# A three-stage fp32 kernel on one core: the first pass ordered by a list scheduler written in the kernel, attention two head pairs at a time

## The chip, the cores and the metric

The kernel runs on one core of a Trainium2 chip. The metric is the device time of one execution in microseconds (us), the median of several. TensorE (PE) multiplies matrices, VectorE (DVE) and ScalarE (ACT) work elementwise, GpSimd (POOL) fills constants, and SyncE (SP) issues nearly all transfers between HBM and the on-chip memory SBUF. PE writes to PSUM, eight banks of accumulators.

## The reference, cut to what matters

A linear attention over 8 batches, 8 heads, 576 tokens and 64 dimensions (softmax of q over the dimensions, softmax of k over the tokens) is followed by two feed-forward layers, 512 to 2048 to 512, over the 4608 tokens. Inputs are 32-bit floats except the weights of the layers, which arrive as 64-bit floats.

```python
q_s = softmax(q, axis=-1)                              # q, k, v: (8, 8, 576, 64)
k_s = softmax(k, axis=2)
kv = np.einsum('bhsd,bhse->bhde', k_s, v)
attn_out = np.einsum('bhsd,bhde->bhse', q_s, kv)
x = attn_out.transpose(0, 2, 1, 3).reshape(4608, 512)
h = x @ w_in                                           # (512, 2048)
x = (h * (1.0 / (1.0 + np.exp(-1.702 * h)))) @ w_out   # (2048, 512)
h = x @ w2_in
g = np.where(h >= 1, h, np.where(h <= -1, 0.0, (h + 1) ** 2 / 4))
return g @ w2_out
```

## The kernel before, in words

Every operand of the large products is split into a high and a low part in the fp32r type (`split`), and a product is three matmuls: high by high, high by low, low by high. The work has four stages: the first pass (attention and `x @ w_in`, activation, result `g0` to HBM), then `out_pass` for the first `w_out` (L308), `pass_in` for the second `w_in` (L463), and `out_pass` again. The last three use a seven-product scheme on quadrants and are not touched, except for two scalings in `post` (L392): the first pass hands on twice the activation, and `keep` and `more` halve it.

The first pass has 9 blocks of 512 tokens and 16 steps a block, 144 steps. Step s is `gemm1` (L794): 12 matmuls of 128x128 by 512 columns for one 128-column slice m of `w_in`. Two steps fill one of two PSUM bank pairs (`hps`); then `act` (L807) runs a Tanh on ACT and a multiply-add on DVE and stores 512 KB of `g0`. In the first 16 steps the weight slices are loaded as 64-bit words and converted (`conv`, one ACT and three DVE instructions; then `split`) into `w_in`, which stays on chip.

Beside the matmuls of block j run the attention pieces of block j + 1 (`chain`, L824). They go by head pair `hp`, four of them: `load_k`, `load_v`, `k_max` (maximum over tokens held on a partition), `k_col` (transpose on PE, maximum on DVE), `k_sub` (transpose back and subtract), `k_exp`, and `k_v`: ten fp32 matmuls that put k'v and the sum of k in the two column halves of one bank, then a scaled copy of two 64x64 blocks into a block-diagonal 128x128 `kv`. For the queries they go by 128 tokens, four tiles a block: `load_q`, `q1` (maximum, subtract), `q1e` (Exp), `q2` (sum, reciprocal, multiply), `q3` (four transposes on PE, a copy to `qT`). `q4` multiplies `qT` of one head pair with `kv`, 512 columns in one or two segments where the block spans two batches, and splits the result into `xh`, `xl`. Block 8 is the last; in block 7 only queries are prepared, since eight batches are done.

From step 17 on, eight sets of the other weights are loaded, converted and turned into the seven combinations that the later stages need (`weight_sets`), one set in 12 steps; the results go to HBM (`wp_*`). Towards the end the first of them come back (`load_weight`), and with block 8 the quadrants of `g0` are loaded for the second pass.

The order: `at(s, f)` notes that piece f is issued after step s; the list is sorted, and the pieces are issued between the steps in that order (L871 on). The framework then orders the instructions of each engine by itself, with priority by this order, so a small matmul can stand in the middle of a step. Every engine runs its instructions strictly in the order that results. The pieces for block 0 come ahead of the first step, q and v of the first two head pairs by ACT's queue, the other loads by SP's.

## Time and profile before

| | us |
|---|---|
| median of 3 runs | 1571.37 |
| lowest and highest | 1567.52, 1572.13 |
| the profiled execution | 1570.93 |
| its span, first to last instruction | 1569.1 |
| its mean granted TensorE clock, as a share of full speed | 0.996 |

The profile is one execution. A page gives the busy time of each engine; the trace behind it is asked for stretches of time, groups of instructions, waits and instructions in order of time. A busy PE is not a PE at its peak, since the ends of matmuls are modelled and they overlap; so the distance between the starts of two matmuls is read, not their length. Where a wait is put down to an instruction, that one came last.

### The profile page before, as it was taken

Reading aid. Unit: us, or ns where it says so; the run is one execution under the profiler, and the core shown is the slowest. Engines: PE = TensorE matmul, PEld = TensorE weight load, DVE = VectorE, ACT = ScalarE, POOL = GpSimd, SP = SyncE. Lnnn points to the kernel's source line nnn. Section 1 sums busy time; section 2 is a strip of 40 time slices with the busy share of each in tenths; the row PEclk is TensorE's granted clock in tenths of the full one; section 3 lists DMA queues with packets and bytes.
Section 4 is the critical chain, followed back from the end, with each engine's and each line's share of the span. In section 5 each row is a group of like instructions: output and inputs, shape, how many; then the busy total and the mean of one; then the engine's idle time right before and its main releaser. Section 6 shows DMA issues by size and latency. Waiting matters only on the chain. (4 is left out here: it accounts for less than half of the span.)

```text
span 1569.1 us, 20971 instructions
## 1 busy us (share of the span) xinstructions
PE 1536.9 (98%) x7748; PEld 1307.6 (83%) x7748; DVE 1163.6 (74%) x1546; ACT 821.9 (52%) x1058; POOL 8.8 (1%) x45
## 2 busy tenths in 40 slices
PE   4999999999999999999999999999999999999998
PEld 2677788777787888888999888888999888888998
DVE  6999887787843678686778577777664879696885
ACT  5555445544523444444445687778776544343442
POOL 0000000000000000000000000000000000000000
PEclk8999999999999999999999999999999999999999
DMA  8787788887787751615268766566744963535341
GB/s 234 212 258 266 263 271 274 267 271 252 251 293 274 289 201 68 213 56 178 71 199 310 294 223 241 202 231 228 259 160 169 426 201 136 159 110 144 111 121 41
DMA packets 249080, 330.65 MB, mean 211 GB/s; under 512 B 129553, under 2 KB 193041, under 8 KB 246289
## 3 DMA queue, kind: packets, MB, share of 16 engines
q1 hardware_dynamic: 243696, 328.09, 62.0%
q10 hardware_dynamic: 5280, 1.21, 0.4%
q8 instruction: 61, 1.00, 0.3%
q14 instruction: 43, 0.34, 0.1%
HBM read 190.84 MB, written 138.41 MB: 210 GB/s over the span
## 5 line engine op out<-in xcount | busy, mean ns | idle before, releaser
L107 ACT ACTIVATE s<-s 128x1024 fp32r<-128x1024 f32 (+2 forms) x363 | 325.1, 901 | 377.9 <-PE z L359 149.7
L108 DVE TENSOR_TENSOR s<-s,s 128x1024 fp32r<-128x1024 f32 (+2 forms) x363 | 369.0, 1023 | 152.7 <-PE zx L359 66.1
L359 PE MATMUL z<-s,w 128*128 128x512 f32 (+1 forms) x1920 | 399.8, 367 | 0.4 <-DVE s L108 0.4
L359 PEld LDWEIGHTS z<-s,w 128*128 128x128 f32 x1920 | 349.5, 188 | 45.9 <-DVE s L108 0.8
L359 PE MATMUL zx<-s,w 128*128 128x512 f32 (+1 forms) x1440 | 300.8, 367 | 0.7 <-DVE s L377 0.7
L359 PEld LDWEIGHTS zx<-s,w 128*128 128x128 f32 x1440 | 262.2, 188 | 34.6 <-DVE s L377 1.0
L803 PE MATMUL hps<-xh,w 128*128 128x512 f32 x576 | 236.2, 410 | 3.0 <-ACT w L107 3.0
L805 PE MATMUL hps<-xh,w 128*128 128x512 f32 x576 | 226.9, 394 | 0.7 <-DVE w L108 0.6
L804 PE MATMUL hps<-xl,w 128*128 128x512 f32 x576 | 226.2, 393 | 0.0
L121 DVE TENSOR_TENSOR s<-s,s 128x1024 f32<-128x1024 f32 (+2 forms) x196 | 204.7, 1058 | 12.7 <-DMA s<-g 8.9
L485 PE MATMUL z<-s,w 128*128 128x512 f32 (+1 forms) x960 | 207.2, 367 | 0.0
L485 PEld LDWEIGHTS z<-s,w 128*128 128x128 f32 x960 | 175.0, 188 | 22.9 <-DVE s L501 0.4
L485 PE MATMUL zx<-s,w 128*128 128x512 f32 (+1 forms) x720 | 158.5, 368 | 1.8 <-DVE s L121 1.6
L485 PEld LDWEIGHTS zx<-s,w 128*128 128x128 f32 x720 | 130.7, 188 | 20.8 <-DVE s L121 3.8
L813 DVE SCALAR_TENSOR_TENSOR sg<-sg,hps 128x1024 f32<-128x1024 f32 x72 | 87.7, 1218 | 62.2 <-ACT sg L812 59.6
L803 PEld LDWEIGHTS hps<-xh,w 128*128 128x128 f32 x576 | 108.8, 189 | 28.8 <-ACT w L107 4.3
L805 PEld LDWEIGHTS hps<-xh,w 128*128 128x128 f32 x576 | 108.2, 188 | 25.6 <-DVE w L108 2.4
L812 ACT ACTIVATE sg<-hps 128x1024 f32<-128x1024 f32 x72 | 73.8, 1025 | 101.4 <-PE hps L805 96.8
L804 PEld LDWEIGHTS hps<-xl,w 128*128 128x128 f32 x576 | 108.5, 188 | 20.9 <-issue 0.6
L500 ACT ACTIVATE s<-s 128x1024 f32<-128x1024 f32 (+1 forms) x80 | 77.6, 971 | 1.6
L499 ACT ACTIVATE s<-s,half 128x1024 f32<-128x1024 f32 (+1 forms) x40 | 42.4, 1060 | 23.6 <-DVE s L121 23.6
L501 DVE SCALAR_TENSOR_TENSOR s<-s,s 128x1024 f32<-128x1024 f32 (+1 forms) x40 | 44.7, 1117 | 12.6 <-ACT s L500 11.2
(79 smaller groups left out, 1074.2 us busy)
## 6 DMA issues: line engine op xcount, KB each, us to landing
s<-g SPq DMA_DIRECT2D x96, 512.0 KB, 5.1
g<-sg SPq DMA_DIRECT2D x72, 512.0 KB, 3.2
w<-wp_out SPq DMA_DIRECT2D x14, 2048.0 KB, 14.8
g<-s SPq DMA_DIRECT2D x48, 512.0 KB, 3.0
s<-g SPq DMA_DIRECT2D x48, 384.0 KB, 4.0
wp_out<-w SPq DMA_DIRECT2D x28, 512.0 KB, 4.0
wp_in<-w SPq DMA_DIRECT2D x28, 512.0 KB, 3.7
w<-wp_in SPq DMA_DIRECT2D x7, 2048.0 KB, 8.7
```

The lines of the kernel that those rows point to most:

```text
L107: first = nc.scalar.activation(out=hi, in_=src, func=ACTF.Copy)
L108: return nc.vector.tensor_tensor(out=lo, in0=src, in1=hi.bitcast(FP32), op=ALU.subtract), first
L121: return nc.vector.tensor_tensor(out=o, in0=x, in1=y, op=op)
L359: nc.tensor.matmul(out=z[:, m, :n], lhsT=a, rhs=b[:, c, :], start=(p in OPENS and i == 0 and c == 0 and x == 0), stop=(i == 3 and c == 1 a ...
L485: nc.tensor.matmul(out=z[:, m, :n], lhsT=a, rhs=b[:, c, :], start=(p in OPENS and c == 0 and x == 0), stop=(c == 1 and x == 2), skip_group ...
L500: nc.scalar.activation(out=t, in_=t, func=ACTF.Square)
L501: nc.vector.scalar_tensor_tensor(out=t, in0=h, scalar=1.0, in1=t, op0=ALU.max, op1=ALU.min)
L803: nc.tensor.matmul(out=hps, lhsT=wh, rhs=xh[:, kk, :], start=(kk == 0), stop=False)
L804: nc.tensor.matmul(out=hps, lhsT=wh, rhs=xl[:, kk, :], start=False, stop=False)
L805: nc.tensor.matmul(out=hps, lhsT=wl, rhs=xh[:, kk, :], start=False, stop=(kk == KD - 1))
L812: nc.scalar.activation(out=sg, in_=hps, func=ACTF.Tanh, scale=0.851)
L813: nc.vector.scalar_tensor_tensor(out=sg, in0=sg, scalar=1.0, in1=hps, op0=ALU.add, op1=ALU.mult)
```

## The change

The pieces of the first pass become entries of a `Plan`: an engine, a price in ns, a rank, names that it reads and writes, bytes' time on the transfer engines (`moves`) and PSUM banks that it takes or gives back. `Plan.order` is a list scheduler: it goes through time, takes on each engine the piece that can start first, and among those the one of lowest rank. The pieces are then issued in that order under `manual_schedule`, so the framework no longer reorders PE, DVE, ACT and SP.

```diff
+class Plan:
+    LATE = {"PE": 190, "DVE": 130, "ACT": 130, "SP": 1900}
+    def __init__(self, banks):
+        self.pieces, self.banks = [], banks
+    def add(self, engine, ns, rank, fn, reads=(), writes=(), moves=0, take=0, give=0):
+        self.pieces.append((rank, len(self.pieces), engine, ns, fn, reads, writes, moves, take, give))
+    def order(self):
+        pieces = sorted(self.pieces, key=lambda x: x[:2])
+        wrote, read, needs, after = {}, {}, [], [[] for _ in pieces]
+        for n, (_, _, _, _, _, reads, writes, _, _, _) in enumerate(pieces):
+            deps = {wrote[r] for r in reads if r in wrote}
+            for w in writes:
+                deps |= {wrote[w]} if w in wrote else set()
+                deps |= set(read.pop(w, ()))
+                wrote[w] = n
+            for r in reads:
+                read.setdefault(r, []).append(n)
+            deps.discard(n)
+            needs.append(len(deps))
+            for d in deps:
+                after[d].append(n)
+        since = [0] * len(pieces)
+        free = dict.fromkeys(self.LATE, 0)
+        open_to = {e: [n for n, x in enumerate(pieces) if x[2] == e and not needs[n]] for e in free}
+        banks, moved, out = [0] * self.banks, 0, []
+        def when(e, n):
+            take = pieces[n][8]
+            if take > len(banks):
+                return None
+            return max(free[e], since[n], sorted(banks)[take - 1] if take else 0)
+        while len(out) < len(pieces):
+            best = None
+            for e, ns in open_to.items():
+                starts = [(t, n) for n in ns if (t := when(e, n)) is not None]
+                if starts:
+                    first = min(t for t, _ in starts)
+                    pick = min(n for t, n in starts if t <= first)
+                    if best is None or first < best[0]:
+                        best = first, e, pick
+            start, e, n = best
+            _, _, _, ns, _, _, _, moves, take, give = pieces[n]
+            open_to[e].remove(n)
+            free[e] = done = start + ns
+            if take:
+                banks = sorted(banks)[take:]
+            if moves:
+                moved = done = max(done, moved) + moves
+            done += self.LATE[e]
+            banks += [done] * give
+            for m in after[n]:
+                since[m] = max(since[m], done)
+                needs[m] -= 1
+                if not needs[m]:
+                    open_to[pieces[m][2]].append(m)
+            out.append((start, n))
+        return [pieces[n][4] for _, n in sorted(out)]
+def now(rank, engine, ns, fn, *_, **__):
+    fn()
```

Attention goes by half the heads (two head pairs, `p`) for k and v and by 256 tokens, two of them on a partition, for q. `k_v` has the same ten matmuls for a head pair, two head pairs in one bank, with the 64 leftover tokens padded to 128 rows; the scaled copy of kv is one DVE instruction, and `kv` is no longer block-diagonal. `q4` has four 64x64 matmuls for two head pairs, in the four quarters of PE's array.

```diff
+        def load_k(b, p, eng=nc.sync):
+            kt = st["k", b, p] = kpool.tile([P, 4, KR + 1, D], FP32, tag="k", name="kt")
+            src = k[b, 4 * p:4 * p + 4]
+            nc.gpsimd.memset(kt[KT:, :, KR], LOWEST)
+            eng.dma_start(out=kt[:, :, :KR], in_=src[:, :KR * P].rearrange("h (p r) d -> p h r d", r=KR))
+            eng.dma_start(out=kt[:KT, :, KR], in_=src[:, KR * P:].rearrange("h p d -> p h d"))
...
+        def k_sub(b, p):
+            kt = st["k", b, p]
+            top = st["pb"].rearrange("p u (h o d) -> p (u h) o d", h=2, o=1)
+            for r0, r1 in ((0, 2), (2, KR + 1)):
+                nc.vector.tensor_tensor(
+                    out=kt[:, :, r0:r1], in0=kt[:, :, r0:r1], in1=top.to_broadcast([P, 4, r1 - r0, D]),
+                    op=ALU.subtract,
+                )
...
+        def k_v(b, p):
+            kt, vt = st["k", b, p], v_t[p]
+            pk = st["pk"] = ps_a.tile([P, 2, D + 1], FP32, tag="a", name="pk")
+            for u in range(2):
+                for r in range(KR + 1):
+                    for h in range(2):
+                        nc.tensor.matmul(
+                            out=pk[h * D:(h + 1) * D, u, :],
+                            lhsT=kt[:, 2 * u + h, r, :],
+                            rhs=vt[:, 2 * u + h, r, :],
+                            start=(r == 0),
+                            stop=(r == KR),
+                            tile_position=(0, h * D),
+                            skip_group_check=True,
+                        )
+        def k_out(b, p):
+            pk = st["pk"]
+            rs = sm.tile([P, 2, 1], FP32, tag="rs", name="rs")
+            nc.vector.tensor_scalar(out=rs, in0=pk[:, :, D:], scalar1=EPS, scalar2=None, op0=ALU.add)
             nc.vector.reciprocal(out=rs, in_=rs)
-            kv = kv_t[b % 2]
-            for j in range(2):
-                o = slice(j * D, (j + 1) * D)
-                nc.scalar.activation(out=kv[o, hp, o], in_=pk[o, :D], func=ACTF.Copy, scale=rs[o])
+            tt(kv_t[b % 2][:, 2 * p:2 * p + 2, :], pk[:, :, :D], rs.to_broadcast([P, 2, D]), ALU.mult)
...
+        def q_exp(t):
+            nc.scalar.activation(out=heads(t), in_=heads(t), func=ACTF.Exp)
...
+        def q4(j, pair):
+            px = [ps_a.tile([P, TB], FP32, tag="a", name="px") for _ in range(2)]
             for off, n, b, s in segs(j * TB, TB, S):
+                for c in range(2):
+                    for r in range(2):
+                        rows = slice(r * D, (r + 1) * D)
+                        nc.tensor.matmul(
+                            out=px[r][c * D:(c + 1) * D, off:off + n],
+                            lhsT=kv_t[b % 2][rows, pair + 2 * c, :],
+                            rhs=st["qT", j][rows, pair + 2 * c, off:off + n],
+                            start=True,
+                            stop=True,
+                            tile_position=(r * D, c * D),
+                            skip_group_check=True,
+                        )
+            for r in range(2):
+                st["px", 2 * pair + r] = px[r]
```

`q1`, `q_exp`, `q2` and `k_max` handle twice the width an instruction. The query and key Exp of a half become one piece, `exps`. The activation becomes one function, and the two scalings of the second pass go:

```diff
         def act(s):
+            sg = st["sg", s] = sgp.tile([P, 2, TB], FP32, tag="sg", name="sg")
+            nc.scalar.activation(out=sg, in_=h_ps[s], func=ACTF.Gelu_apprx_sigmoid)
...
-            nc.scalar.activation(out=sg, in_=hps, func=ACTF.Tanh, scale=0.851)
-            nc.vector.scalar_tensor_tensor(
-                out=sg, in0=sg, scalar=1.0, in1=hps, op0=ALU.add, op1=ALU.mult
-            )
-            nc.sync.dma_start(out=g0_dram[j][m // 2], in_=sg)
```

The order of heads in x changes, so a weight slice is loaded with two transfers of 64 partitions. The pieces, with their ranks and prices:

```diff
+        def attention(j, c0):
             b = j if j < B else None
...
+                put(-5, "SP", 560 * (2 if j else 1), lambda t=t: load_q(t), step(u - 6), nf, moves=1750)
...
+                    put(-6, "SP", 1120, lambda p=p: load_k(b, p), step(u - 7), nk, moves=1800)
+                    put(-1, "SP", 2800, lambda p=p: load_v(b, p), step(u - 2), nv, moves=2600)
+                    put(0, "DVE", 1350, lambda p=p: k_max(b, p), nk, ("mx",))
+                    put(1, "PE", 230, k_col, ("mx",), ("pa",), take=1)
+                    put(1.2, "DVE", 350, k_top, ("pa",), ("mc",), give=1)
+                    put(2, "PE", 230, k_row, ("mc",), ("pb",), take=1)
+                    put(2.2, "DVE", 1500, lambda p=p: k_sub(b, p), ("pb",), nk, give=1)
+                    put(5, "PE", 1400, lambda p=p: k_v(b, p), nk + nv, ("pk",), take=1)
+                    put(5.2, "DVE", 500, lambda p=p: k_out(b, p), ("pk",), (("kv", b % 2, p),), give=1)
+                put(0.2, "DVE", 2400, lambda t=t: q1(t), nf, nq)
+                def exps(t=t, p=p):
+                    q_exp(t)
+                    if b is not None:
+                        k_exp(b, p)
+                put(3, "ACT", (1000 + (1200 if b is not None else 0)) + (2560 if j else 0), exps, (),
+                    nq + (nk if b is not None else ()))
+                put(4.2, "DVE", 2650, lambda t=t: q2(t), (), nq)
+                for r in range(2):
+                    put(6, "PE", 480, lambda t=t, r=r: q3(t, r), nq, (("pt", r),), take=1)
+                    put(6, "ACT", 520, lambda t=t, r=r: q_out(t, r), (("pt", r),), (("qT", p, r),), give=1)
+            qT = tuple(("qT", p, r) for p in range(2) for r in range(2))
+            kv = tuple(("kv", bb, p) for bb in range(2) for p in range(2))
+            for pair in range(2):
+                add("PE", 1000, c0 + 12, lambda pair=pair: q4(j, pair), qT + kv, (("px", pair),), take=2)
+                for r in range(2):
+                    c = 2 * pair + r
+                    add("ACT", 530, c0 + 12.5, lambda c=c: x_hi(j, c), (("px", pair),), (("xh", x, c),))
+                    add("DVE", 620, c0 + 12.6, lambda c=c: x_lo(j, c), (("px", pair), ("xh", x, c)),
+                        (("xl", x, c),), give=1)
+        for m in range(NM):
+            weight(m)
+        for j in range(NB):
+            attention(j, (j - 1) * NM)
...
+        room = (("room", 0),)
+        add("PE", 0, s0 - 0.01, last_block,
+            step(s0 - 1) + tuple((n, 0, c) for n in ("xh", "xl") for c in range(4)), room)
+        for rank, fn in (
+            (0, lambda: g0.load(0, "11")), (4, lambda: g0.load(0, "12")), (8, lambda: g0.load(0, "22")),
+            (14, lambda: load_weight(w_out1, "out1", 2)), (14.1, lambda: g0.load(0, "21")),
+        ):
+            add("SP", 1300, s0 + rank, fn, room + step(s0 + int(rank) - 1), (), moves=5000)
...
+            add("DVE", 1300, s0 + 13 + i, lambda i=i: ready0(i), room + step(s0 + 11 + i), ())
+        for s in range(NB * NM):
+            j, m = divmod(s, NM)
+            hb, gb = ("hps", s // 2 % 2), ("sg", s // 2 % 3)
+            x = tuple((n, j % 2, c) for n in ("xh", "xl") for c in range(4))
+            add("PE", 2720, s, lambda s=s: gemm1(s), x + (("wh", m), ("w", m)) + (room if j == NB - 1 else ()),
+                (hb,) + step(s))
+            if s % 2:
+                add("ACT", 950, s + 1.05, lambda s=s: act(s), (hb,), (gb,))
+                add("SP", 420, s + 1.6, lambda s=s: store_g(s), (gb,), (), moves=1270)
...
+        engines = {mybir.EngineType.PE, mybir.EngineType.DVE, mybir.EngineType.Activation, mybir.EngineType.SP}
+        with tc.manual_schedule(engines=engines):
+            for fn in plan.order():
+                fn()
```

The prices of `conv`, of the weight sets and of the weights' splits follow the same manner. Weight sets come every 14 steps (`s0 = NM + 1 + 14 * i`), each gated by the step two before its rank; the first three combinations of the first `w_out` come back at ranks 130, 133 and 136 (before: after step 113). All loads of block 0 go by SP's queue. GpSimd no longer clears `kv` and pads one k tile for two head pairs.

## Rows read from the trace of the kernel before

**Rows 1.** The page, part 1: busy time, share of the span, instructions.
```profile
PE 1536.9 (98%) x7748; PEld 1307.6 (83%) x7748; DVE 1163.6 (74%) x1546; ACT 821.9 (52%) x1058; POOL 8.8 (1%) x45
```

**Rows 2.** Stretches, cut where a block's first matmul starts; columns in the first line.
```profile
core 0: us, PE busy (x) PEld busy (x) DVE busy (x) ACT busy (x) POOL busy (x), PEclk, DMA share, GB/s
0.00:40.11 40.11, 18.91 (x113) 11.17 (x113) 26.01 (x69) 21.32 (x62) 3.55 (x21) 0.83 0.87 236
40.11:101.26 61.15, 57.51 (x314) 43.17 (x313) 59.36 (x120) 35.59 (x59) 0.80 (x4) 1.00 0.78 234
...
210.29:264.64 54.35, 54.35 (x313) 43.82 (x312) 43.40 (x78) 27.32 (x41) 1.24 (x4) 1.00 0.82 267
...
430.58:479.54 48.96, 48.96 (x217) 38.99 (x216) 23.64 (x36) 15.31 (x20) 0.00 (x0) 1.00 0.70 254
479.54:523.08 43.54, 43.54 (x194) 36.04 (x193) 12.13 (x10) 10.23 (x10) 0.00 (x0) 1.00 0.92 326
```

**Rows 3.** Waits of PE, 40 to 530 us: us in total, times, longest.
```profile
PE hps L803 <- ACT w L107: 3.0, 4, 1.2
```

**Rows 4.** PE in order of time, end of block 7: start, us, what.
```profile
473.10 0.60 PE L764 MATMUL pt<-ident,qt 128*128 128x128 f32 x4
474.47 3.62 PE L774 MATMUL px<-qT,kv 128*128 128x512 f32 x8
```

**Rows 5.** PE in order of time, a k chain between matmuls of block 0.
```profile
57.17 0.39 PE L805 MATMUL hps<-xh,w 128*128 128x512 f32 x1
57.48 0.95 PE L709 MATMUL pk<-v,kt 128*64 128x65 f32 x20
58.37 0.33 PE L681 MATMUL pa<-ident,mx 128*128 128x128 f32 x1
58.45 0.48 PE L803 MATMUL hps<-xh,w 128*128 128x512 f32 x1
58.77 0.40 PE L804 MATMUL hps<-xl,w 128*128 128x512 f32 x1
```

**Rows 6.** Groups of ACT instructions by form: busy us, mean ns, idle before.
```profile
L812 ACT ACTIVATE sg<-hps 128x1024 f32<-128x1024 f32 x72 | 73.8, 1025 | 101.4 <-PE hps L805 96.8 <-DMA g<-sg 4.2
...
L700 ACT ACTIVATE kt<-kt 128x640 f32<-128x640 f32 x32 | 23.6, 737 | 21.0 <-DVE kt L691 20.4
...
L724 ACT ACTIVATE kv<-pk,rs 64x64 f32<-64x64 f32 x64 | 19.6, 307 | 23.9 <-DVE rs L720 19.6 <-DVE qz L753 3.9
...
L745 ACT ACT_TABLE_LOAD x1 | 1.3, 1283 | 9.4 <-DMA qt<-in_q_dram 9.4
```

**Rows 7.** Groups of DVE instructions by form.
```profile
L813 DVE SCALAR_TENSOR_TENSOR sg<-sg,hps 128x1024 f32<-128x1024 f32 x72 | 87.7, 1218 | 62.2 <-ACT sg L812 59.6 <-DMA wp_in<-w 1.6 <-DMA g<-sg 0.9
...
L108 DVE TENSOR_TENSOR w<-w 128x512 fp32r<-128x512 f32 x64 | 43.5, 683 | 1.4 <-ACT w L107 1.3
...
L755 DVE TENSOR_TENSOR qt<-qt,qz 128x512 f32<-128x512 f32 x36 | 24.7, 687 | 0.3
```

**Rows 8.** The start in order of time: first DVE pass, `q4`, first matmul.
```profile
3.83 0.42 DVE L673 TENSOR_TENSOR m<-kr 128x256 f32<-128x256 f32 x1 [3.83 <-DMA kr<-in_k_dram]
...
34.41 6.26 PE L774 MATMUL px<-qT,kv 128*128 128x512 f32 x8 [0.88 <-ACT qT L769]
40.11 0.79 PE L803 MATMUL hps<-xh,w 128*128 128x512 f32 x1
```

**Rows 9.** Three more stretches: ahead of the first matmul, and around the seam.
```profile
30.00:40.00 10.00, 9.12 (x35) 4.93 (x36) 6.70 (x16) 5.30 (x11) 0.00 (x0) 0.52 0.92 254
...
460.00:480.00 20.00, 20.00 (x86) 15.03 (x85) 12.06 (x19) 8.08 (x12) 0.00 (x0) 1.00 0.35 132
...
540.00:560.00 20.00, 20.00 (x90) 16.55 (x89) 15.42 (x14) 9.90 (x10) 0.00 (x0) 1.00 0.08 32
```

**Rows 10.** DMA issues by group: count, KB each, median us to landing.
```profile
g<-sg SPq DMA_DIRECT2D x72, 512.0 KB, 3.2
```

450 lines of the change are left out of this document (178 added, 272 removed).

## The prediction

> **What bounds the kernel now.** First the page's busy table: TensorE (PE) is busy 98% of the span [rows 1], so a gain has to shorten PE's own stream or its start. Next the stretches of the first pass, cut at the first matmul of each block [rows 2]. A block is 16 steps of 12 matmuls, 192 in all. The last block has nothing beside them and lasts 43.54 us, 0.227 us a matmul: that is the floor. Block 7, with only the query side of attention beside it, lasts 48.96; block 3, with everything, 54.35; block 0 lasts 61.15, with VectorE (DVE) busy for 59.36 of it. Before the first matmul lie 40.11 us. After the pass (from 523.08 us) the diff changes nothing but two scalings. So all that can be won lies in the first 523 us: 40.11 of start, 6.8 that block 0 is longer than block 3, and some 10.8 a block in which PE does attention. The waits of PE inside the pass are small: 3.0 us for converted weights is the longest entry [rows 3].
>
> **The change part by part.** The sum is made against the profiled execution, 1570.93 us (span 1569.1 and 1.8 around it); the median of the runs is 1571.37, so a difference carries over as it is.
>
> *Attention on PE, blocks 1 to 7.* Block 7 has 5.42 us above the floor for four groups of query transposes and `q4`. `q4` there is eight records in 3.62 us, two for each of four matmuls, 0.45 each [rows 4]; the transposes are then 0.45 a group. Block 3 less block 7 is 5.39 for four k chains, 1.35 each. Of a chain, `k_v` starts 0.08 after a matmul could have, its 20 records take 0.89 to the start of `k_col`, and the matmul after next starts at 58.77 instead of 57.62: 1.15 for both [rows 5], and 0.2 is left for `k_row`.
> After: the transposes are the same 16. The k chains keep their 80 `k_v` records at 0.045 each, in two groups, not four: 2 x (1.8 + 0.15) and four entries of `k_col` and `k_row` at 0.2 make 4.7 instead of 5.4, a gain of 0.7 (bounds 0 and 1.2). `q4` is now 16 records a block of the same width, each on a quarter of the array. If the four quarters run side by side, 16 x 0.45 / 4 = 1.8; one after the other, 7.2. The nearest row is `k_v`: its two column halves alternate, and a record takes 0.045, although 65 columns at the rate of `q4` (0.45 x 65/512) are 0.057. So neighbours in different tiles do overlap. I take 1.8, with 0.2 to enter and leave each of two groups: 2.2, a gain of 1.4. Together 2.1 a block.
>
> *ScalarE (ACT).* `act` becomes one instruction instead of one on ACT and one on DVE; I price Gelu at Tanh's 1.025 [rows 6]. The trace has one table load, 1.283 us: Tanh and Exp needed no other. The plan charges 2.56 us to each `exps` piece, two loads, for going to Exp and back; two pieces a block. A piece is then 1.28 + 1.03 + 1.3 (query and key exps; the latter is 0.737 at half the width), and the next `act` 1.28 + 1.03 after it: 5.9 us. PE has 5.45 us (two steps) until it needs the bank that `act` empties, so only a piece that starts just ahead of an `act` holds PE, by 0.5, plus what else is queued; behind it on ACT stand `x_hi`, `q_out` and the next `act`. Bounds 0 to 1.2 a block; I take 0.5. In total ACT is busy 27 of 54 us [rows 2], eight kv copies of 0.307 go, four loads come: some 30.
> What the Trainium skill says in "ScalarE: Activation LUTs", section "What ACT_TABLE_LOAD costs", speaks against this part: a switch costs about 2.66 us with the drain around the load, not the load alone. The trace has no switch in mid-stream to test it; by that figure the two switches would be 5.3, and the piece and its `act` 8.7, so up to 3 us of PE wait a piece in the worst place.
>
> *DVE.* Block 3 has 43.4 us of DVE work [rows 2]. Eight multiplies of `act` at 1.218 go (9.7) [rows 7]. Query passes go from 12 at 0.687 to 6 at 1.22 (0.9 less), weight sets (some 17 passes, 14 us) come every 14 steps instead of 12 (2.6 less): about 30 remain, and DVE sets nothing in blocks 1 to 7.
>
> *Blocks 1 to 7 in sum:* -2.1 + 0.5 = -1.6 each in blocks 1 to 6, -9.6. Block 7, without k chains: -1.4.
>
> *Block 0.* It needs 16 weight conversions (one pass of half width and three of 0.68 as [rows 7] has them, about 2.5 us each, 40 in all) and the attention of block 1 (about 21). Without the multiplies, and with some 9 us of conversions done in the start, DVE has about 52 us of work against PE's 43.5 + 9. The 6.8 us shrink to about 3 (DVE and PE are level, and conversion m has to be there at step m), and PE's attention saves its 1.6. I take -5.6; bounds 0 and -8.
>
> *The start.* All loads are on SP's queue now; q and v of the first pieces no longer go out from ACT. By rank SP issues k, q, v of the first half, then of the second: 3.4 MB, then a third k before the first weight. At the 236 GB/s of the first 40 us [rows 2] the six land at about 5.6, 8, 10.5, 13, 15 and 18. (Before, the first DVE pass began at 3.83 on a quarter of the heads [rows 8]; waiting for half of them costs 1.5 us here.) The chain of the second half, by row durations: q landed 15; `q1` 2.4; `q2` of the first half 2.7 and `k_sub` 1.6 to 22; `exps` to 24.5; `q2` 2.7 to 27; transposes and `q_out` to 30. `q4` began at 34.41 in the trace, and its eight records took until 40.11, 0.71 each [rows 8], at a granted clock of 0.52 from 30 to 40 us, the 1.2 GHz level [rows 9]; PE had mostly been waiting before. At the same clock and with four quarters side by side it is about 3.5 instead of 5.7: first matmul at 34 to 35. Against that, a DVE piece that already runs (up to 2.7 us; pieces are twice as long as before) can stand in the way of the chain. I take -5; bounds -8 and +3.
>
> *The seam to the second pass.* The weight sets end later (at step 129, before at 117) and three w_out1 loads of 2 MB move from block 7 into block 8, on SP between the g0 loads that the second pass begins with. Block 8 moved 326 GB/s at a DMA share of 0.92 [rows 2]; 460 to 480 us had 0.35 and 540 to 560 us 0.08 [rows 9]. 6 MB more at 326 GB/s are 18 us, and the idle stretch after 540 takes them; the quadrants of the second product are needed about 11 us after the seam. That cover is thin: 0 to +8, and +2 in the sum, with the plan's other slips.
>
> *At nothing:* the key tile's padding by GpSimd, longer DMA rows for q, two half-height issues for each of 16 weights, fewer copies of kv. The issues hide behind landings; without that cover each would cost its issue on SP, once, in the start or in block 0.
>
> Sum: -5 - 5.6 - 9.6 - 1.4 + 2 = -19.6; 1570.93 - 19.6, about 1551 us.
>
> **The rivals.** *Quarters overlap only with their neighbour.* Every fp32 matmul is two records on the same quarter. If records start strictly in order, the second waits for the first (0.45), and only then may the next quarter begin: one matmul every 0.45 us, eight a block, and one more 0.45 for each group's end: 4.5 + 0.4 instead of 3.62. `k_v` fits this as well as the forecast, for it has only two tiles. Then `q4` costs +1.3 instead of -1.4: blocks 1 to 6 +1.1 each, block 7 +1.3; the start saves 1.5, for `q4` takes 8 us at 1.2 GHz; block 0 saves 3.5. Sum: 6.6 + 1.3 - 1.5 - 3.5 + 2 = +4.9, 1576 us, at the edge of no change.
> This is what a rule of the Trainium skill gives, "TensorE: Matmul & The Clock Gate", Part 3, "What overlaps and what doesn't": matmuls start and end in program order. The trace has no group of four tiles to test it.
>
> *Row halves don't overlap.* `k_v` shows overlap for column halves alone; no row shows it for row halves, and the loop changes rows first. `q4` would be 7.2 + 0.4, +4 a block: blocks 1 to 6 +3.8, block 7 +4, the start +1.3 (11.4 us of cold `q4`, begun 4.4 earlier), block 0 -1, slips 2: +29, 1600 us, slower. The sign turns where `q4` takes more than 4.2 us a block: 19.6 spread over seven blocks, block 0 and the cold start, 9.6 times, on top of 2.2.
>
> *The written order slips.* Engines go strictly in the order that the plan fixes with its own prices; a 512 KB store counts 1.27 us there, while it took 3.2 to land [rows 10] and DMA is already at 0.8 in block 3 [rows 2]. If SP sits on a store whose `act` is late, k, q and v behind it come late, then DVE and PE. Against it: PE's prices in the plan are 51 us a block, mine 53, so the others should wait for PE. At 4 us for each of eight blocks the gain turns to +12, 1583 us.
>
> **How the numbers follow.** Forecast 1551 (its own spread 1540 to 1562): 0.54. Neighbours only, 1576: 0.22. Order slips, 1583: 0.12. Row halves, 1600: 0.08. A larger gain, below 1538, if ACT holds nothing and the start reaches its bound: 0.04. About 0.3%, 4.7 us, is what a measurement of this kernel can tell from no change. Faster: 0.53 + 0.04 + a little of the second case, 0.60. Same: almost half of the second case, edges of the first and third, 0.14. Slower: the rest, 0.26. The range 1538 to 1580 leaves out most of the slips, the row-halves case and the tail below.
>
> **What would show it.** `q4`: 16 records in about 2 us a block (forecast), 4.5 (neighbours), 7.2 (row halves). First matmul at 34 to 35 us; block 0 about 55.5, blocks 1 to 6 about 52.8, block 7 47.5, block 8 43.5. Table loads about 33, and no PE wait on ACT above 1 us. DVE busy some 30 us a block. No PE wait on a DMA between 523 and 560 us. The prediction is wrong if blocks 1 to 6 stay at 54 or more, if PE waits for DVE or ACT pieces by several us a block, or if the second pass gets longer.

## The result, and the profile after

| | before | after |
|---|---|---|
| median of 4 runs, us | 1571.75 | 1553.51 |
| lowest to highest, us | 1567.52 to 1572.70 | 1550.85 to 1554.19 |
| span of the profiled execution, us | 1569.1 | 1550.9 |

The ratio is 0.9886, with a 95% interval of 0.9865 to 0.9907: faster by 1.1%, 18.2 us by the medians; the forecast was 1551.

Where the 18.2 us of the span are, by the first matmul of each block (read from PE in order of time in the one traced execution, as in [rows 2]):

| stretch | before | after | difference | forecast |
|---|---|---|---|---|
| start, to the first matmul | 40.11 | 39.42 | -0.7 | -5 |
| block 0 | 61.15 | 59.44 | -1.7 | -5.6 |
| blocks 1 to 6 | 329.32 | 312.73 | -16.6 | -9.6 |
| block 7 | 48.96 | 47.62 | -1.3 | -1.4 |
| block 8 | 43.54 | 44.43 | +0.9 | 0 |
| the later stages | 1046.0 | 1047.3 | +1.3 | +2 with the slips |

The sum was right and two of its terms were not: the first 99 us gave 2.4 instead of 10.6, and blocks 1 to 6 gave 16.6 instead of 9.6.

The page of after, part 1, answers [rows 1]:

```profile
PE 1508.9 (97%) x7876; PEld 1293.5 (83%) x7876; DVE 1079.3 (70%) x1288; ACT 827.5 (53%) x961; POOL 6.4 (0%) x27
```

DVE lost 84 us of work; ACT gained 6, since it has 32 table loads instead of one and the copies of kv went [rows 6]. The stretches of after, columns as in [rows 2] (start, block 0, 1, 4, 7, 8):

```profile
0.00:39.42 39.42, 16.17 (x165) 11.17 (x165) 29.63 (x49) 15.68 (x21) 2.88 (x16) 1.00 1.01 224
39.42:98.86 59.44, 52.99 (x291) 41.40 (x289) 55.19 (x98) 37.70 (x51) 0.80 (x2) 0.97 0.94 245
98.86:150.44 51.58, 51.58 (x330) 41.62 (x328) 32.80 (x52) 27.78 (x34) 0.61 (x2) 1.00 0.73 232
...
254.73:308.99 54.26, 51.82 (x329) 41.72 (x328) 40.00 (x59) 28.66 (x36) 0.61 (x2) 1.00 0.88 280
411.59:459.21 47.62, 47.62 (x225) 38.07 (x224) 20.52 (x28) 21.71 (x29) 0.00 (x0) 1.00 0.73 276
459.21:503.63 44.42, 44.42 (x197) 36.80 (x196) 2.45 (x2) 10.10 (x10) 0.00 (x0) 1.00 1.01 395
```

Blocks 1, 2 and 5 are all 51.57 or 51.58 with PE busy throughout; block 0 has PE idle for 6.5 us and DVE busy for 55.19 of 59.44; blocks 3 and 4 are 1.15 and 2.7 longer than their neighbours. The waits of PE from 40 to 530 us (in total, times, longest), to set beside [rows 3]:

```profile
PE pt L840 <- DVE qt L193: 6.3, 3, 3.3
PE pa L764 <- DVE mx L193: 2.1, 1, 2.1
PE hps L893 <- ACT sg L899: 0.4, 1, 0.4
```

There is no wait on ACT above 0.4 us. One of the table loads, ACT in order of time in block 0:

```profile
59.45 0.62 ACT L716 ACTIVATE w<-w 128x512 fp32r<-128x512 f32 x1
60.09 1.28 ACT L824 ACT_TABLE_LOAD   x1
61.39 1.07 ACT L824 ACTIVATE qt<-qt 128x1024 f32<-128x1024 f32 x1
```

From the end of the activation ahead to the start of the next are 1.31 us: this switch costs the load of 1.283 and next to nothing more. There are 32 loads, 16 to Exp and 16 back. One opens the program; the other 15 to Exp are all alike in this, and of those back three. The rest of those back have idle time beside them, most of it until PE is done with the bank that the activation reads. The Trainium skill gives 2.66 us a switch ("ScalarE: Activation LUTs", "What ACT_TABLE_LOAD costs"); the trace does not agree, and the measurement decides.

### The profile page after: what moved, and what is told of

Its sections match the earlier page's. It is cut to its first block, busy times and chain, and to the rows that moved or that the text cites. A ratio compares the mean times of both kernels' runs of the same rounds, so it can differ in the third digit from the quotient of the medians.

```text
span 1550.9 us, 20716 instructions
## 1 busy us (share of the span) xinstructions
PE 1508.9 (97%) x7876; PEld 1293.5 (83%) x7876; DVE 1079.3 (70%) x1288; ACT 827.5 (53%) x961; POOL 6.4 (0%) x27
## 4 chain that ended last, share of the span: by engine, by line
PE 85%; DVE 6%; DMA 6%; ACT 2%; issue 1%; SPq 0%; DVEq 0%; ACTq 0%
PE z L448 25%; PE zx L448 19%; PE z L569 9%; PE hps L893 7%; PE hps L895 7%; PE hps L894 7%; PE zx L569 7%; DMA s<-in_moe_w_out_dram 2%; DVE s L193 1%; PE px L857 1%; PE pt L840 1%; PE pk L796 1%; DMA wp_out<-s 1%; DMA qf<-in_q_dram 1%; DMA w<-in_moe_w_in_dram 1%
## 5 line engine op out<-in xcount | busy, mean ns | idle before, releaser
L179 ACT ACTIVATE s<-s 128x1024 fp32r<-128x1024 f32 (+1 forms) x315 | 306.1, 976 | 365.7 <-PE zx L448 144.1
L180 DVE TENSOR_TENSOR s<-s,s 128x1024 fp32r<-128x1024 f32 (+1 forms) x315 | 349.6, 1115 | 194.3 <-PE zx L448 66.3
L193 DVE TENSOR_TENSOR s<-s,s 128x1024 f32<-128x1024 f32 (+3 forms) x244 | 223.2, 932 | 17.5 <-DMA s<-g 7.1
L893 PE MATMUL hps<-xh,w 128*128 128x512 f32 x576 | 231.5, 402 | 0.4 <-ACT sg L899 0.4
L895 PE MATMUL hps<-xh,w 128*128 128x512 f32 x576 | 225.4, 391 | 0.0
L193 DVE TENSOR_TENSOR w<-w 128x512 fp32r<-128x512 f32 (+1 forms) x96 | 64.0, 686 | 18.2 <-ACT w L257 14.8
L585 DVE SCALAR_TENSOR_TENSOR s<-s,s 128x1024 f32<-128x1024 f32 (+1 forms) x40 | 44.7, 1117 | 12.6 <-ACT s L584 12.1
```

The source lines that it names most:

```text
L179: first = nc.scalar.activation(out=hi, in_=src, func=ACTF.Copy)
L180: return nc.vector.tensor_tensor(out=lo, in0=src, in1=hi.bitcast(FP32), op=ALU.subtract), first
L193: return nc.vector.tensor_tensor(out=o, in0=x, in1=y, op=op)
L585: nc.vector.scalar_tensor_tensor(out=t, in0=h, scalar=1.0, in1=t, op0=ALU.max, op1=ALU.min)
L893: nc.tensor.matmul(out=hps, lhsT=wh, rhs=xh[:, kk, :], start=(kk == 0), stop=False)
L895: nc.tensor.matmul(out=hps, lhsT=wl, rhs=xh[:, kk, :], start=False, stop=(kk == KD - 1))
```

## The experiments

All have the edit made in the changed kernel, unless said otherwise. The times of the first pass, read as above from the one traced execution of each; "end" is the end of block 0 from the span's start, the last column the ratio to the kernel before, run on the same chip (none where there was a single execution). Ratios that lie within some 0.003 of each other are not told apart by their intervals; the readings go by the block times, which come back to a few hundredths where nothing was touched (51.57, 51.03, 47.62):

| kernel | start | block 0 | end | blocks 1 to 7 | us | ratio |
|---|---|---|---|---|---|---|
| before | 40.1 | 61.2 | 101.3 | 54.8 54.3 54.4 54.5 55.2 56.3 49.0 | 1571.75 | |
| after | 39.4 | 59.4 | 98.9 | 51.6 51.6 52.7 54.3 51.6 51.0 47.6 | 1553.51 | 0.9886 |
| `q4` whole | 45.0 | 54.3 | 99.3 | 52.9 52.9 54.4 53.5 52.9 52.8 49.0 | 1559.45 | 0.9934 |
| Tanh back | 40.6 | 63.8 | 104.4 | 52.4 51.6 52.5 51.8 51.7 52.5 47.0 | 1557.09 | 0.9914 |
| Gelu alone | 39.6 | 58.9 | 98.5 | 54.4 54.3 54.4 55.4 55.3 62.9 49.1 | 1574.90 | 1.0027 |
| free order | 34.8 | 74.4 | 109.1 | 51.6 51.6 51.6 51.6 51.6 51.0 47.6 | 1556.86 | 0.9920 |
| fixed to step 15 | 40.9 | 58.0 | 98.9 | 52.6 52.0 51.6 51.6 51.6 51.0 47.6 | 1550.02 | 0.9870 |
| half of w_in | 38.8 | 59.6 | 98.4 | 51.6 51.6 51.6 53.9 51.6 51.0 47.6 | 1550.65 | |
| weights first | 37.5 | 60.8 | 98.3 | 51.6 51.6 53.0 53.4 51.6 51.0 47.6 | 1550.77 | 0.9874 |
| low part on GpSimd | 47.0 | 53.8 | 100.8 | 51.6 51.6 51.6 55.5 51.6 51.0 47.6 | 1554.61 | 0.9898 |
| no low part | 45.1 | 50.7 | 95.8 | 51.6 51.6 51.6 55.6 51.6 51.0 47.6 | 1549.93 | |
| low words on ACT | 42.7 | 53.0 | 95.7 | 51.8 52.3 51.8 56.0 51.8 51.9 47.5 | 1561.08 | 0.9938 |
| first, and fixed to 15 | 36.8 | 60.8 | 97.6 | 51.6 53.0 53.1 51.6 51.6 51.0 47.6 | 1552.02 | 0.9875 |
| words on ACT, fixed to 15 | 41.8 | 53.5 | 95.3 | 53.4 51.6 51.6 51.6 51.6 51.0 47.6 | 1546.24 | 0.9832 |

### Do the four quarters overlap? `q4` over the whole array again

```diff
-                for c in range(2):
-                    for r in range(2):
-                        rows = slice(r * D, (r + 1) * D)
...
-                            tile_position=(r * D, c * D),
+                for r in range(2):
+                    nc.tensor.matmul(
+                        out=px[r][:, off:off + n],
+                        lhsT=kv_t[b % 2][:, 2 * pair + r, :],
```

(`kv` is block-diagonal again; the rest stays.)

> The changed kernel with q4 alone put back to one 128x128 matmul a head pair (kv block-diagonal again, k_out in two halves, the plan's price for a q4 piece 1900 ns). Theory (four quarters side by side carry half of the gain of a block): q4 goes from 16 records in 2.0 us to 8 records at 0.45, 3.6 us a block, so blocks 1 to 7 and block 0 are 1.6 us longer each, the start some 2 us: 1553.5 + 13 to 15 = about 1567. Rival (the gain of blocks 1 to 7 comes from grouping k_v and from the relief of VectorE, and q4 is a small part): under +4 us, below 1558.

The same place in both traces, PE in block 1, where the columns come in segments of 384 and 128: first after, then `q4` whole.

```profile
136.98 1.96 PE L857 MATMUL px<-qT,kv 64*64 64x128 f32 x32
```

```profile
137.36 3.64 PE L857 MATMUL px<-qT,kv 128*128 128x128 f32 x16
```

Twice the records in 1.96 instead of 3.64 us, for the same columns. Four quarters do run side by side, rows as well as columns. The rival of neighbours (4.5 and more) and that of the row halves (7.2) are both out. Over the quiet blocks 1, 2 and 5 the quarters are worth 1.33 us each (52.9 against 51.57), the forecast's 1.4, and 1.4 in block 7. The whole came 5.9 us longer, not the 13 to 15 that were expected: the quarters are worth 1.33 a block and not 1.6, block 8 and the later stages took 2.7 less in its trace, and the start grew by 5.6 while block 0 shrank by 5.1. So the end of block 0 moved by 0.5 only: the first sign that the first 99 us as a whole are set by something else.

### Gelu and its table loads: Tanh put back, and Gelu alone in the kernel before

```diff
-            nc.scalar.activation(out=sg, in_=h_ps[s], func=ACTF.Gelu_apprx_sigmoid)
+            nc.scalar.activation(out=sg, in_=h_ps[s], func=ACTF.Tanh, scale=0.851)
...
+                add("DVE", 1140, s + 1.3, lambda s=s: act2(s), (hb,), (gb,))
```

> The changed kernel with the activation alone put back: Tanh on ScalarE and the multiply-add on VectorE as a piece of the plan (1140 ns), the doubled activation halved in the second pass, no table loads charged to exps. Theory (blocks 1 to 7 are bound by PE, only start and block 0 by VectorE): blocks 1 to 6 stay at 51.6 us with VectorE at 43 of them; block 0 gets longer by 4 to 8 us, since seven multiplies of 1.22 us come on top of 55 busy of 59: about 1559. Rival (VectorE's relief is what shortened blocks 1 to 6 beyond the forecast of 1.6 each): 1.2 us or more a block on top, 1567 or more. The third way, that 32 table loads held PE: faster than 1553.

The table loads fell from 32 to 1, and blocks 1 to 6 are no faster for it (312.6 us in sum against 312.7): the loads cost PE nothing there, and the quiet blocks are 51.6 in both. Block 0 grew by 4.3, and most of PE's waiting there is now for the multiply that was put back on DVE:

```profile
PE hps L898 <- DVE sg L907: 6.5, 3, 3.7
```

PE had idled nearly as long in the changed kernel, though, on other pieces: 6.5 us in block 0, and 7.5 here. The other 3.3 of the 4.3 us are busy time of PE (56.3 against 53.0), at a granted clock of 0.91 instead of 0.97 over the block; it was 0.59 from 55 to 60 us and 0.68 from 95 to 100, where PE had just stood 3.7 and 2.0 us on the multiply. So Gelu's worth lies ahead of block 1, where DVE is short: 5.5 us at the end of block 0, the clock's part included.

In the kernel before, the converse edit (Gelu for Tanh and multiply, and the two scalings of `post`):

> The kernel before with one part of the change alone: the one-function activation in place of Tanh and the multiply, and the second pass without the halving. Theory (two table loads of 1.3 us for every Exp that stands alone; 8 Exp pieces a block): up to 16 loads, 21 us of ScalarE a block on top of 27 of 54, so ScalarE comes near its limit and PE waits for a PSUM bank in some steps: blocks 1 to 6 at 54 to 58, 1570 to 1595. Rival (PE never waits for ScalarE, and VectorE's 9.7 us less a block shorten block 0): block 0 at 56, the others as before, about 1566.

The end of block 0 moved from 101.3 to 98.5, about as far as with the whole change (98.9). But the kernel was slower as a whole (1.0027, interval 1.0015 to 1.0039). The framework's order loads tables 84 times. Blocks 1 to 5 took hardly longer for it (273.8 us in sum, before 273.1), but block 6 took 62.9 instead of 56.3. There ACT had a table load, a Gelu and a weight's copy ahead of the copy to `qT` for which PE's `q4` was waiting:

```profile
424.78 1.28 ACT L807 ACT_TABLE_LOAD   x1 [0.98 <-issue]
426.07 1.02 ACT L807 ACTIVATE sg<-hps 128x1024 f32<-128x1024 f32 x1
427.12 0.63 ACT L107 ACTIVATE w<-w 128x512 fp32r<-128x512 f32 x1
427.66 0.58 ACT L764 ACTIVATE qT<-pt 128x512 f32<-128x512 f32 x1
```

```profile
428.29 7.10 PE L769 MATMUL px<-qT,kv 128*128 128x448 f32 x16 [2.73 <-ACT qT L764]
```

PE stood idle for 2.73 us, and the granted clock was 0.56 from 428 to 435.2 us, near its 1.2 GHz level; `q4` took 7.10 instead of 3.62 [rows 4]. So a table load did have a part in a wait of PE here, unlike in the changed kernel. In the old order Gelu gains nothing; whether an order that keeps the Exps together would have been enough there was not tested.

### What the fixed order does: a free order, and one that is fixed to step 15 only

```diff
-        with tc.manual_schedule(engines=engines):
-            for fn in plan.order():
-                fn()
+        for fn in plan.order():
+            fn()
```

> The changed kernel with the pieces traced in the plan's order, but the framework orders each engine's instructions itself, as in the kernel before. Theory (the order within an engine matters where VectorE is nearly full, in the start and block 0, and not in blocks 1 to 7): within 4 us of 1553.5, blocks 1 to 6 at 51 to 53, the difference ahead of 100 us. Rival (the strict order is what gives the gain, by keeping PE's small matmuls together): blocks 1 to 6 at 53 to 54.5, 1565 or more.

The start of this kernel is the forecast's: `q4` from 30.87 and the first matmul at 34.75 (PE in order of time).

```profile
30.87 3.95 PE L857 MATMUL px<-qT,kv 64*64 64x512 f32 x16 [0.19 <-ACT qT L847]
34.75 0.50 PE L893 MATMUL hps<-xh,w 128*128 128x512 f32 x1
```

Block 0 then took 74.35, with PE waiting in the steps for converted weights (waits from 34 to 110 us). The waits are 11.2 us of it (6.5 in the changed kernel); PE was also busy for 63.1 instead of 53.0, with 334 matmul records instead of 291, since pieces of block 1 that the fixed order has in the start fall into this block, and at a granted clock of 0.93 instead of 0.97:

```profile
PE hps L893 <- ACT w L716: 7.8, 5, 3.0
PE hps L895 <- DVE w L193: 2.3, 3, 1.5
```

Blocks 1 to 5 were 51.57 to 51.59 without a slip. So the slips of blocks 3 and 4 in the changed kernel come from the fixed order: loads that come late, then DVE, then PE, as in the rival, at a small price. There, SP and then DVE in order of time:

```profile
242.86 3.54 SPq L742 DMA_DIRECT2D v<-in_v_dram  x1
...
248.58 1.20 SPq L733 DMA_DIRECT2D kt<-in_k_dram  x1
```

```profile
205.14 0.69 DVE L193 TENSOR_TENSOR m<-kt 128x512 f32<-128x512 f32 x1 [6.83 <-DMA kt<-in_k_dram]
...
206.72 1.22 DVE L829 TENSOR_REDUCE qz<-qt 128x16 f32<-128x1024 f32 x1
...
255.32 0.69 DVE L193 TENSOR_TENSOR m<-kt 128x512 f32<-128x512 f32 x1 [3.16 <-DMA kt<-in_k_dram]
...
256.90 1.22 DVE L174 SCALAR_TENSOR_TENSOR w<-w 128x1024 uint32<-128x1024 uint32 x1
```

In block 3 DVE stands 6.83 us on k, with query passes (`L829`) that need no k in the queue behind; PE then waits 0.60 us for them, at 209.75. In block 4 it stands 3.16 us, with a weight pass (`L174`) behind, and then 0.77 for a query load; PE waits 2.44 us for the query passes, at 264.31. A fixed queue cannot step past. In the kernel fixed to step 15 the last query pass of that place came ahead of k's:

```profile
200.38 1.22 DVE L193 TENSOR_TENSOR qt<-qt,qz 128x1024 f32<-128x1024 f32 x1
...
202.64 0.68 DVE L193 TENSOR_TENSOR m<-kt 128x512 f32<-128x512 f32 x1
```

A wait on k alone is no slip: in the free order DVE once stood 5.06 us on k (until 298.67), and that block has none. Ahead of block 4 the transfers were full, with a share of 1.06 from 234 to 246.4 us; a v load issued at 234.35 landed 12.6 later, SP was held 5.2 and 3.5 us in issuing two pieces of v, and three stores and then k's load stand behind them. It was not PE that held SP, since PE's last reading of the old v (`k_v`, 225.22) was long done; what did is not shown beyond the full transfers.

The plan's order for the first 16 steps (`n` is the place of step 16's `gemm1`), and the framework's freedom behind them:

```diff
+        order = plan.order()
+...
+        with tc.manual_schedule(engines=engines):
+            for fn in order[:n]:
+                fn()
+        for fn in order[n:]:
+            fn()
```

> The plan's order is fixed by hand up to step 15 (start and block 0) and given to the framework as a priority only from step 16 on. If the fixed order costs in the start nothing and in blocks 3 and 4 the slips of 1.15 and 2.7 us (query passes behind a late transfer): end of block 0 at 98.9, blocks 1 to 6 at 51.57 each, run about 1549.5. If the framework's freedom brings other delays, as it did in block 0 where it ran throughout (74 us): some block above 53, run at 1553 or more.

1550.02 us (0.9870, 0.9853 to 0.9886), against 1549.5 expected: the slips of blocks 3 and 4 are gone, and 1.5 us come back in blocks 1 and 2, where the order changes hands.

### What sets the first 99 us

Transfers had a share of 0.94 in block 0, DVE was busy for 93% of it, and the greedy list puts block 1's pieces into the start. Four kernels tell these apart. The first leaves out half the rows of each `w_in` slice (zeros stand in their place), so that 4.2 MB less are moved:

```diff
-            for c in range(2):
+            for c in range(1):
                 nc.sync.dma_start(
```

> Leaves out the second half of the rows of each w_in slice's load (zeros stand in the buffer), so 4.2 MB of some 23 MB that are to move ahead of the end of block 0 don't; the order, the passes and the products stay. If the transfers set the first 99 us, the end of block 0 comes at 85 to 92 instead of 98.9; if VectorE's passes or the fixed order set them, at 96 to 99. Later blocks unchanged, 51.6 us each with at most two slips.

98.4: half a microsecond, with the transfers' share in block 0 down to 0.68. Not the transfers, then, as far as one execution tells. The second gives the weights' pieces an earlier rank:

```diff
-                add(engine, ns, m - 3 + k, fn, reads, writes)
+                add(engine, ns, m - 6 + k, fn, reads, writes)
```

> One number of the plan: the pieces of a w_in slice get the rank m - 6 instead of m - 3, so they come ahead of more of block 1's attention. By the plan's own timetable block 1 begins at 90.0 instead of 91.6 and the first matmul at 36.1 instead of 37.9. If the list order is what stands in the chain of the first 99 us: first matmul about 1.5 earlier, the gaps of block 0 (3.3 and 6.7 us ahead of steps whose weights came late) mostly gone, end of block 0 at 93 to 96, run 1548 to 1551. If the amount of VectorE or DMA work sets it: end of block 0 within 1 us of 98.9, for the amount is the same.

The first matmul came 1.9 earlier, as expected, but the end of block 0 only 0.6: what the start won, PE waited for in block 0 (3.4 us on `xh` of the other head pairs, 2.3 on an activation). By what was expected, this is the answer for the amount of work and not for the order. The third moves one pass of each slice from DVE to GpSimd:

```diff
-            put(1, "DVE", 620, lambda: tt(lo, f, hi.bitcast(FP32), ALU.subtract), nq + (("wh", m),), nw)
+            put(1, "POOL", 1200, lambda: nc.gpsimd.tensor_tensor(
+                out=lo, in0=f, in1=hi.bitcast(FP32), op=ALU.subtract
+            ), nq + (("wh", m),), nw)
```

> The low part of each of the sixteen w_in slices (f minus hi) goes from VectorE to GpSimd, as a piece of the plan; nothing else changes. It takes sixteen passes of about 0.6 us, some 9.6 us, off VectorE ahead of the end of block 0. Theory A, VectorE sets the first 99 us (it is busy 93% of block 0): the end of block 0 comes 5 to 9 us earlier, at 90 to 94, and the run takes about 1545. Theory B, the transfers set them (DMA share 0.94 there): end of block 0 within 2 us of 98.9, run 1552 to 1554. Theory C, the fixed order sets them, and a late piece on one engine holds up the others: between 94 and 98, by the chance of the new order. Blocks 1 to 8 as before in all of them.

The end moved the wrong way, to 100.8. By the number that is theory B, which the halved loads exclude. The first 99 us of after and of this kernel (columns as in [rows 2]):

```profile
0.00:99.00 99.00, 69.30 (x453) 52.70 (x454) 84.97 (x146) 53.51 (x71) 3.68 (x18) 0.98 0.97 237
```

```profile
0.00:99.00 99.00, 66.76 (x444) 51.52 (x445) 84.41 (x127) 50.88 (x70) 27.50 (x34) 0.93 0.92 224
```

DVE has 19 instructions less and is just as busy: 84.41 us against 84.97. Its other passes became slower. The same groups, 41 to 99 us, in after and then with GpSimd at work (busy us, mean ns, idle):

```profile
L171 DVE SCALAR_TENSOR_TENSOR w<-w 128x512 uint32<-128x512 uint32 x13 | 8.9, 686 | 0.0
L174 DVE SCALAR_TENSOR_TENSOR w<-w 128x512 uint32<-128x512 uint32 x13 | 8.9, 686 | 0.0
L168 DVE TENSOR_SCALAR w<-w 128x512 uint32<-128x512 uint32 x12 | 5.0, 422 | 0.0
```

```profile
L174 DVE SCALAR_TENSOR_TENSOR w<-w 128x512 uint32<-128x512 uint32 x13 | 10.7, 825 | 0.1
L171 DVE SCALAR_TENSOR_TENSOR w<-w 128x512 uint32<-128x512 uint32 x12 | 9.6, 806 | 0.0
L168 DVE TENSOR_SCALAR w<-w 128x512 uint32<-128x512 uint32 x12 | 7.6, 648 | 0.5 <-DMA w<-in_moe_w_in_dram 0.5
...
L717 POOL TENSOR_TENSOR w<-w 128x512 fp32r<-128x512 f32 x14 | 21.4, 1541 | 29.0 <-ACT w L716 28.9
```

The means rose from 686 to 825 and 806, and from 422 to 648 ns. The Trainium skill names a cause ("Trainium Architecture — The Big Picture", "What this means for kernel authors"): VectorE and GpSimd share one pair of SBUF ports, and whichever holds it locks the other out. The trace agrees in that DVE's passes slowed, by the means above; that it was a lock, no row shows. So this kernel took nothing off DVE and says nothing on whether DVE is the bound. The fourth therefore leaves the low parts out altogether (GpSimd fills them with zeros):

```diff
-            put(1, "DVE", 620, lambda: tt(lo, f, hi.bitcast(FP32), ALU.subtract), nq + (("wh", m),), nw)
+            nc.gpsimd.memset(w_in[m // 4][:, 1, m % 4, :].bitcast(FP32), 0.0)
```

> Leaves out the low part of the sixteen w_in slices (GpSimd fills it with zeros, a short fill a slice), so VectorE has sixteen passes of 0.6 to 0.69 us, some 10 us, less ahead of the end of block 0, and no GpSimd arithmetic runs beside it as it did when the pass was moved there. If the amount of VectorE work sets the first 99 us (it is busy 85 us of them, and starts only when the first data lands): end of block 0 at 90 to 94 instead of 98.9. If a chain through other engines or the fixed order sets it: 96 to 99. By the plan's own timetable block 1 would begin 2.5 us earlier.

The end came at 95.8, 3.1 earlier, in its one execution: between the two answers. The rows show why it is not more. PE does not wait in block 0 any more (50.67 us, less than block 1), but its first matmul comes only at 45.09 (PE in order of time):

```profile
33.42 1.94 PE L857 MATMUL px<-qT,kv 64*64 64x512 f32 x14 [0.29 <-DVE kt L781]
37.78 2.34 PE L796 MATMUL pk<-v,kt 128*64 128x65 f32 x40 [2.42 <-ACT kt L788]
43.50 1.94 PE L840 MATMUL pt<-ident,qt 128*128 128x128 f32 x8 [3.38 <-DVE qt L193]
45.09 0.78 PE L893 MATMUL hps<-xh,w 128*128 128x512 f32 x1
```

`q4` is done at 35.4, and ahead of the first step stand `k_v` and the transposes of block 1, with what they wait for. So both have a part in the first 99 us: the amount of DVE's work (3.1 us for ten taken away, 5.5 for the 8.5 that Tanh's multiply adds), and the list's order, which lets block 1's pieces go ahead of block 0's first step. How much each is worth these kernels do not separate, for the granted clock moved too: over the start it was 0.83 before, 1.00 in after, 0.85 with Tanh, 0.86 with the weights first and 0.81 without the low part, where the transposes at 43.50 took 1.94 us at 0.50 (1.09 in block 3 of after at 1.00). An order with the early start of the free kernel (34.75) and a block 0 without waits was not found.

### A pass that ACT can take, and the fastest version

ACT is busy for 38 of block 0's 59 us. It can take the pass on the low words (422 ns on DVE), with a small bias in place of the minimum:

```diff
+        if low:
+            put(0, "ACT", 60 + 0.92 * n, lambda: nc.scalar.activation(
+                out=r, in_=lw, func=ACTF.Relu, scale=2.0 ** -29, bias=under
+            ), na, nr)
...
+    under = const.tile([P, 96], FP32, name="under")[:, :1]
```

> The pass of a w_in slice that scales the low words (128x512, 0.42 us on VectorE beside the others) goes to ScalarE as one activation, some 0.6 us there; sixteen passes, 6.8 us less on VectorE and about 9 more on ScalarE, which is busy 38 of 59 us in block 0. If VectorE's amount sets the first 99 us: end of block 0 3 to 6 us earlier, 93 to 96, run 1547 to 1551. If not: within 1.5 us of 98.9, run 1552 to 1555; if ScalarE with its table loads becomes the late one, PE waits for ACT pieces in block 0 and the end comes after 99. Blocks 1 to 8 unchanged.

The end of block 0 came at 95.7, 3.2 earlier, and the whole was 7.6 us slower. The loss lies elsewhere: the later stages took 1054.5 instead of 1047.3, and in block 8, where PE does next to nothing but the steps' matmuls, they stand 0.229 and 0.237 apart in turn, 0.233 in the mean of the block:

```profile
487.70 0.39 PE L902 MATMUL hps<-xh,w 128*128 128x512 f32 x1
487.93 0.40 PE L900 MATMUL hps<-xh,w 128*128 128x512 f32 x1
488.17 0.39 PE L901 MATMUL hps<-xl,w 128*128 128x512 f32 x1
```

[Rows 2] have 0.227 for that block, and so has every other kernel here. The granted clock was 1.00 in it, so that is not the cause. The new constant's tile of 96 columns, 384 bytes a partition, moves what is laid out behind it in SBUF; the addresses themselves stand in no row. Before that was tested, one kernel joined the two edits of the order that had each shortened the run by the medians (their intervals overlap with that of the changed kernel):

> The two edits that each made the run shorter, together: rank m - 6 for the pieces of a w_in slice, and the order fixed only up to step 15. If the two gains are in different places (the end of the start and block 0 by the one, the slips of blocks 3 and 4 by the other): end of block 0 at 98.3, blocks 1 and 2 at 52 to 52.6, blocks 3 to 6 at 51.57, run about 1549. If block 0's end does not depend on the rank at all: 1550, as with the order alone.

1552.02 us, 0.9875 (0.9858 to 0.9891): no better than either alone. In the traced execution, at 1548.50 the fastest of its four, the end of block 0 won 1.3 against the order fixed to step 15 and block 1 another 1.0, and blocks 2 and 3 lost 2.4. The last kernel has the pass on ACT, its constant in an unused column of a tile that is there already, and the order fixed to step 15:

```diff
-    half = const.tile([P, 96], FP32, name="half")[:, :1]
+    spare = const.tile([P, 96], FP32, name="half")
+    half, under = spare[:, :1], spare[:, 1:2]
```

> Two things together: the low-word pass of a w_in slice on ScalarE, as in the run before, but with its bias constant in an unused column of a tile that is there already, so that no address of SBUF moves; and the order fixed only up to step 15. In the run before every second matmul of the last block stood 0.233 us after the one ahead instead of 0.227, and the three later stages took 1054.5 instead of 1047.3 us. If the moved addresses did that: spacing back at 0.227 and the later stages at 1046 to 1047; if ScalarE's added passes or table did it: spacing still 0.233. If VectorE's amount sets the first 99 us in part: end of block 0 at 95 to 96, blocks 1 and 2 at 52 to 52.6, blocks 3 to 6 at 51.57, run 1545 to 1548, the fastest so far; if the shorter block 0 came from moved addresses too (hardly): 98.9 and 1550.

```profile
487.68 0.39 PE L900 MATMUL hps<-xh,w 128*128 128x512 f32 x1
487.90 0.39 PE L901 MATMUL hps<-xl,w 128*128 128x512 f32 x1
488.13 0.39 PE L902 MATMUL hps<-xh,w 128*128 128x512 f32 x1
```

The mean of the block is 0.227 again, and the later stages are back at 1047.0: with no tile added, ACT's sixteen passes cost nothing there. The order also differs between these two kernels, but the changed kernel and the one fixed to step 15 have it both ways at 0.227; so by elimination the moved addresses are what is left, though no kernel moved them alone. Which tile's it was, and why blocks 1 to 7 hardly show it, is open. The end of block 0 is 95.3, the whole 1546.24 us, ratio 0.9832 (0.9813 to 0.9851), below the interval of the changed kernel (0.9865 to 0.9907): the fastest of all.

## Why the prediction held, step by step

*Attention on PE, blocks 1 to 7.* `q4`: forecast 1.4, measured 1.33 a block (the whole-array run) and 1.4 in block 7; the four quarters run side by side. In the start its 16 records took 1.07 and 1.94 us, at a granted clock of 1.00 from 30 to 40 us, not at the 0.52 of [rows 9]; what I priced at 1.2 GHz ran at 2.4. In the free order, at 0.54 from 30 to 35 us, the same 16 took 3.95. The k chains were the mis-sized term: I had 0.7, and with `q4` whole the quiet blocks still gained 1.45 (54.35 to 52.90; part of it may be other parts of the change, which no run took out there). By what stands between the step matmuls of block 2, 10.7 us became 8.0. The two groups of `k_v` add 2.82 where I had 3.9 (40 records in 1.39, not 1.8), and `k_col` and `k_row` 0.56 where I had 0.8. The step matmuls with nothing ahead of them come late too, nearly all of it just behind an interruption, by 2.2 us in sum before and 1.07 after: there were 15 interruptions a block and are 9, and that I had not counted.

*ACT.* Forecast +0.5 a block, measured none: a switch is 1.31 us, PE waits 0.4 us in all for activations, and the run with Tanh shows blocks 1 to 6 no faster. That is six times 0.5 of the 7 us by which blocks 1 to 6 beat the forecast; the k chains are six times 0.75. Blocks 5 and 6 of before were also 0.9 and 1.9 longer than block 3, on which I had worked, and that went too; the slips in blocks 3 and 4 took 3.8 back.

*DVE.* Some 30 us a block forecast; 32.8 in block 1, 40 in block 4. It sets nothing there but the slips.

*The start: the step that failed.* My chain ran to the end of `q4` and took that for the first matmul. `q4` itself began at 32.36, some 2 us behind my chain, and was done at 35.7; it would have been later at the clock that I had priced, so this end is in part luck. (DVE's first pass began at 5.13, 1.3 later than in [rows 8], as expected.) But ACT then had the Exps of block 1 ahead of the second `x_hi`, and DVE weights ahead of the second `xl`:

```profile
34.86 1.08 ACT L876 ACTIVATE xh<-px 128x512 fp32r<-128x512 f32 x2 [2.05 <-PE px L857]
35.83 1.06 ACT L824 ACTIVATE qt<-qt 128x1024 f32<-128x1024 f32 x1
36.77 1.27 ACT L788 ACTIVATE kt<-kt 128x1280 f32<-128x1280 f32 x1
37.94 1.08 ACT L876 ACTIVATE xh<-px 128x512 fp32r<-128x512 f32 x2
```

```profile
38.10 1.39 PE L796 MATMUL pk<-v,kt 128*64 128x65 f32 x40 [2.41 <-ACT kt L788]
39.42 0.50 PE L893 MATMUL hps<-xh,w 128*128 128x512 f32 x1
...
41.71 0.50 PE L894 MATMUL hps<-xl,w 128*128 128x512 f32 x1 [0.41 <-DVE xl L193]
```

PE, too, stood 2.41 us for a `k_v` of block 1 that the list had put ahead of the first step. The order is readable in the code before any run: the scheduler takes what can start first, and rank decides only among pieces that can start at the same time. The free order had its first matmul at 34.75, and paid for it in block 0.

*Block 0.* Forecast -5.6, measured -1.7. "DVE and PE are level" was right as far as it went, but I took start and block 0 as two gains. DVE did 85.4 us of work by the end of block 0 before (26.01 and 59.36, [rows 2]) and 84.8 after (29.63 and 55.19), in 101.3 and 98.9 us: what it no longer multiplies, it does of other pieces sooner. Such a stretch has one end, and the start could not be won on top of it. The runs show this bound in part only (3.1 us for 10 of DVE's); the order has a part in the rest, and how much the clock has is open.

*Block 7.* -1.4 forecast, -1.34 measured.

*The seam.* +2 forecast, +2.2 measured: 0.9 in block 8, where four matmuls of the next stage now stand ahead of the last steps, and 1.3 behind it. That they agree is luck: block 8 and what follows take 1088.5 to 1091.7 us in the thirteen kernels other than the one with the added tile, 1089.6 before and 1091.7 after. The only wait of PE on a DMA in the later stages, on weights that come back, is 0.5 us.

*The order slips.* The rival's 4 us a block came as 1.15 and 2.7 in two of eight. The loads were late behind full transfers, and not, as the rival had it, behind a store whose `act` was late.

So 1551 against 1553.51 is a right mechanism for `q4`, and two errors of 7 and 8 us that cancel by luck.

## What to carry to other kernels

Small fp32 matmuls of 64x64 can be laid on the four quarters of the array and run side by side; fewer, larger groups between the steps save as well, because each interruption costs the matmul behind it. When an engine is busy for nearly all of a stretch, the stretch as a whole has one gain, not one for each of its parts: sum the busy time first. A greedy list that takes what can start first lets later work stand ahead of the critical piece, and an order fixed to the end cannot step past a late transfer: fix it where many engines must meet, and leave the rest free.
